# Two moves in a fused attention and MLP kernel: low bits of the weights go from ScalarE to GpSimd, block copies go to more steps

## The chip, the cores and the metric

The kernel runs on one core of a Trainium2 chip. The metric is the device time of one execution, in microseconds (us), as a median of runs. The core's engines run side by side and each takes its own instructions strictly in order: TensorE (PE, with its weight loads, PEld), VectorE (DVE), ScalarE (ACT), GpSimd (POOL), and SyncE (SP), which here only issues DMAs. Before the change the median of three runs is 744.94 us (744.84 to 745.29).

## The reference, cut to what matters

Block-sparse attention over four batches, eight heads, 768 positions, head size 64, and behind it an MLP with squared ReLU over the 3072 tokens.

```python
block, n_blocks, window = 32, 24, 1
scores = scale * np.matmul(q, k.transpose(0, 1, 3, 2))
mask = np.abs(blk_i - blk_j) <= window
mask = mask | (blk_i == 0) | (blk_j == 0) | (blk_i == n_blocks - 1) | (blk_j == n_blocks - 1)
# ... and 3 sampled key blocks for each query block
attn = softmax(where(mask, scores, -1e9));  x = attn @ v
h = np.maximum(x @ w_in, 0.0)          # (3072 x 512) @ (512 x 2048)
return (h * h @ w_out).astype(np.float32)
```

Two things matter here. The first and the last query block see all keys ("whole rows"); the others see a few blocks. And the weights w_in and w_out arrive as float64: each is two 32-bit words, from which the kernel makes fp32 itself.

## The kernel before, in words

The 3072 tokens go through the MLP in eight chunks of 384, and each chunk passes over the 16 blocks f of the hidden dimension. For each f `hidden(c, f)` does twelve matmuls into ph (L883): x and the weight are each cut into a high and a low part, wi holds both parts of the weight, and three products are added. The squared ReLU makes gh and its low part gl (L904 to L917) on ACT, DVE and POOL; `project(c, f)` follows two f later with nine matmuls into po (L936), which need gh, gl and wo. In chunk 0 the projection is plain fp32, three matmuls that the trace shows as six records (L926), and needs only WO and gp.

Between these matmuls stands the attention of the next chunk's tokens, cut into units which are generators: each `yield` hands over to the next step, and a table of lags (`LAG`) says how many steps lie between a unit's parts. A unit of whole rows (class Whole) exists for the batches after the first; twelve of them run, four within each of chunks 1, 3 and 5. Its parts are scores, maxima, exps (pg), the block copies (`move`, L660: sixteen copies of 32x192 elements pg → pgm, even ones by POOL, odd ones by ACT), one transpose by VectorE (L666, pgm → pTg) and the values (pvg, L694). The program's order is each engine's order: no scheduler moves instructions afterwards.

Chunk 0 also makes the weights. For every f and both matrices (part 0 is w_in, which becomes W; part 1 is w_out, which becomes WO) `cut_next` takes four stages in turn, one call every three steps of chunk 0:

- `cut_load` (L785): POOL issues the DMA of 128x1024 32-bit words into craw
- `cut`: ACT makes the rounded top word (L801) and the low bits: it reads the upper 16-bit half of each low word, scales it and writes an integer over the low word (L803)
- `cut_bits`: VectorE shifts and joins both (L812), then the sign (L813); with that W or WO is complete and craw is free
- `cut_split` for a few f only

`split` (L845, L848) makes wi: ACT casts W to the high part (in chunk 0; VectorE in later chunks, L847), and POOL subtracts for the low part. Raw words craw, wi, wo, pg and pgm rotate through one set of seven buffers (tag "w"), so that a new wi waits until an older tenant of its buffer is done; in the middle of chunk 0 that is a craw which `cut_bits` of WO has read. In that stretch ACT, DVE and POOL also carry the attention's exps, maxima (L448), transposed copies (pT), normalisation (rec, xn) and copies of keys into place (L290, L308, L338).

The names in the order of instructions are tile, chunk and f: wi0_7 is wi of chunk 0, f=7; craw8_1 is the raw block of f=8, part 1; pgm1_3 is a unit of whole rows of batch 1.

Of the kernel before, what the change touches and what calls it, by code (L numbers as in the profile page):

```python
# [14 lines left out]
AF = mybir.ActivationFunctionType  # L15
ALU = mybir.AluOpType
# [46 lines left out]
STEP = PIECES // (2 * UC)  # L63
EARLY = 23
LAST = 4
LAG = {"s": 0, "e": 4, "v": 11, "x": 4, "t": 4, "c": 0, "v0": 13, "w0": 4, "w": 19, "n": -1}

G_AT = 6

# [1 line left out]
STEP_1, FIRST_1 = 12, 0  # L71
LAG_1 = {**LAG, "v": 10, "x": 3, "t": 6, "v0": 5, "n": 0}
LAG_0 = {"s": 2, "x": 2, "t": 3, "c": 2, "v0": 2, "n": 2, "r": 1, "l": 3, "l0": 8}
# [23 lines left out]
def tile_block_sparse_attention_moe(ctx: ExitStack, tc, kd, knd, qd, qgd, vd, vnd, samp, const, wcat, out):  # L97
# [9 lines left out]
    nc = tc.nc  # L107
# [14 lines left out]
    below = one.tile([P, 1], F32, name="below")  # L122
# [46 lines left out]
    pool = {}  # L169
# [183 lines left out]
    def load_sampled(k, u, eng, on, which=range(NRAND)):  # L353
        us = halves(k, u)
        if us is None:
            return
        b, t = order[k]
        VA, VB = values_of(k)
        vals = sampled(t, 1, on)
        v4 = columns(vd[b], us).rearrange("(a p) u c -> p a u c", p=BLK)  # L360
        for j in sorted(groups(t)):
            for r in which:
                a = (place(k, j, 3) if r == 2 else 2 + r) * BLK
                dst = (VB if r == 2 else VA)[a : a + BLK, us, j]
                eng.dma_start(dst.unsqueeze(1), v4[:, bass.ds(vals[NRAND * j + r], 1)])
# [215 lines left out]
    class Whole:  # L581
# [71 lines left out]
        def move(self):  # L653

            self.pm = rot.tile([P, NJ, NT, BLK], F32, tag="w", name=f"pgm{self.name}", bufs=WBUFS)
            x = self.p.rearrange("p (k a s) -> p k a s", k=NT, a=NJ)
            for g in range(NJ):
                for a in range(NJ):
                    copy = nc.scalar.copy if a % 2 else nc.gpsimd.tensor_copy
                    copy(self.pm[a * BLK : (a + 1) * BLK, g], x[g * BLK : (g + 1) * BLK, :, a])  # L660
                    if a % 2:
                        yield 0

        def turn_blocks(self):
# [57 lines left out]
    def units(c):  # L722

        halves = [Half(b, t, u) for b, t in order[c * UC : (c + 1) * UC] for u in range(2)]
        wholes = [] if c % 2 else [Whole(c // 2, pr) for pr in range(NPAIR)]
        if c == 0:
            return [(i * STEP_0, u) for i, u in enumerate(wholes + halves)]
        if c == 1:
            return [(i * STEP_1 + FIRST_1, u) for i, u in enumerate(halves)]
        at = begins(c - 1) - EARLY  # L730
        both = [(at + i * STEP, u) for i, u in enumerate(halves)]
        both += [(at + i * STEP + G_AT, u) for i, u in enumerate(wholes)]
        return sorted(both, key=lambda x: x[0])
# [43 lines left out]
    def whole_block(f, part):  # L777
        if part:
            return WO[f]
        return W1[f] if f in SINGLE else rot.tile([P, DM], F32, tag="x", name=f"ct{f}", bufs=5)  # L780

    def cut_load(f, part):
        if wide:
            cv[f, part] = rot.tile([P, DM, 2], I32, tag="w", name=f"craw{f}_{part}", bufs=WBUFS)
            nc.gpsimd.dma_start(cv[f, part].rearrange("p a b -> p (a b)"), wcat[f, part].bitcast(I32))  # L785

    def cut(f, part):

        t = whole_block(f, part)
        if not wide:
            nc.gpsimd.dma_start(t, wcat[f, part])
            cv[f, part] = t
            return
        raw = cv[f, part]  # L800
        nc.scalar.mul(t, raw[:, :, 1].bitcast(F32), 2.0**-112)  # L801
        top = raw.bitcast(U16).rearrange("p a (b c) -> p a b c", c=2)[:, :, 0, 1]
        nc.scalar.activation(raw[:, :, 0], top, AF.Identity, scale=2.0**-13, bias=below)  # L803
        cv[f, part] = raw, t

    def cut_bits(f, part):
# [22 lines left out]
    def cut_next():  # L829

        nonlocal done
        n = len(cuts)
        for stage, lag in ((cut, AHEAD), (cut_bits, AHEAD + 1), (cut_split, AHEAD + 2), (cut_load, 0)):
            if 0 <= done - lag < n:
                stage(*cuts[done - lag])
        done += 1
# [5 lines left out]
    def split(c, src, name):  # L842
        w = rot.tile([P, 2, DM], F32R, tag="w", name=name, bufs=WBUFS)
        if c == 0:
            nc.scalar.copy(w[:, 0], src)  # L845
        else:
            nc.vector.tensor_copy(w[:, 0], src)  # L847
        nc.gpsimd.tensor_tensor(w[:, 1], src, w[:, 0], op=ALU.subtract)  # L848
        return w
# [176 lines left out]
    def prepare():  # L1026
        for k in range(1, UC):
            key_windows(k, 1, nc.vector.tensor_copy)
        for _ in range(AHEAD):
            cut_next()  # L1030
        deque(first, 0)
        for f in windows(1, 0) + windows(1, 1):
            f(nc.gpsimd.tensor_copy)
        load_sampled(1, 0, nc.sync, SP, (2,))
        load_sampled(2, 1, nc.sync, SP, (0, 1))
        deque(copy_keys(0, 2), 0)
# [8 lines left out]
    while work.todo or work.running:  # L1045
        work.step(now)
        now += 1
        ahead = ahead or (later[0] if later else None)
        if now >= KEYS_1 and now % KEYS_N == 0 and later and later[0] is ahead and next(ahead, True):
            later.pop(0)  # L1050
        if now >= FIXED_0 and fixed:
            fixed.pop(0)(nc.scalar.copy)
            if not fixed:
                load_sampled(2, 1, nc.sync, SP, (2,))
        if now == KEYS_0:
            prepare()
        if now >= CUT_0[0] and (now - CUT_0[0]) % CUT_0[1] == 0:
            cut_next()
        if now == SPLIT_0:
            wi1[0, 1] = split(0, W1[1], "wi0_1")  # L1060
    start.__exit__(None, None, None)
    pool["x"] = ctx.enter_context(tc.tile_pool(name="moe", bufs=2, reuse_waits="tile"))
    W1.update({f: pool["x"].tile([P, DM], F32, name=f"W1{f}", bufs=1) for f in SINGLE if f >= W1_LOW})
    WO.update({f: pool["x"].tile([P, DM], F32, name=f"WO{f}", bufs=1) for f in range(WO_LOW, NF)})
    for c in range(1, NCH):
        for at, u in units(c):
            work.add(at, c, lambda u=u, lag=LAG_1 if c == 1 else LAG: u.run(bank, lag))
    now = 0
# [71 lines left out]
```

## Time and profile before

| what | value |
|---|---|
| median of three runs | 744.94 us (744.84 to 745.29) |
| the profiled execution | 745.86 us |
| span of its instructions | 744.0 us |
| TensorE clock granted, mean | 0.991 |
| busy: PE / DVE / ACT / POOL | 714.0 / 533.0 / 500.5 / 539.4 us |
| low bits on ACT (L803) | 32 times, 24.9 us |
| block copies (L660) | 96 on POOL, 36.7 us; 96 on ACT, 33.6 us |
| chunk 0's matmuls | from about 60 to 165 us |

In the profile's rows an arrow reads "out<-in"; a number in square brackets is the idle time of the engine ahead of the row and what ended it. Matmuls overlap each other in the pipeline, so that twelve rows of 0.35 us take about 2.1 us together. "Issue" in the chain of waits is time in which an engine waited for nothing that the profile shows.

### The profile page before, as it was taken

How to read it: one execution, taken by the hardware profiler on the slowest of the kernel's cores; microseconds unless marked ns; L12 is line 12 of the kernel's file. 1: busy time of each engine (PE TensorE's matmuls, PEld its weight loads, DVE VectorE, ACT ScalarE, POOL GpSimd, SP SyncE). 2: the span in 40 equal slices, each digit the busy share in tenths (PEclk: the TensorE clock that was granted, in tenths of full speed). 3: DMA queues.
4: the chain of work that ended last, by engine and by line, in shares of the span. 5: the costliest groups of instructions: out<-in, count | busy, mean ns of one | idle time of the engine just before them, and what ended most of it. 6: DMA issues, size and time to landing. Idle time of an engine off the chain costs nothing.

```text
span 744.0 us, 21519 instructions
## 1 busy us (share of the span) xinstructions
PE 714.0 (96%) x7496; PEld 569.7 (77%) x7496; DVE 533.0 (72%) x1076; ACT 500.5 (67%) x1107; POOL 539.4 (73%) x681
## 2 busy tenths in 40 slices
PE   5869999999999999999999999999999999999997
PEld 2546666567878888877878888877778888888996
DVE  7885766968776877768877786768778686647552
ACT  5875677998875875579776777478866776623222
POOL 7986734249786587769877577877976586868985
PEclk9988999999999999999999999999999999999999
DMA  8785799755555547645455466455355452101001
GB/s 271 226 225 159 206 298 304 179 154 171 146 126 130 174 126 211 145 104 144 104 165 146 100 193 177 132 131 176 95 160 143 100 160 55 34 1 44 1 1 42
DMA packets 94479, 105.22 MB, mean 141 GB/s; under 512 B 13827, under 2 KB 82180, under 8 KB 94372
## 3 DMA queue, kind: packets, MB, share of 16 engines
q1 hardware_dynamic: 88420, 81.00, 41.1%
q0 software_dynamic: 5664, 22.45, 9.2%
q8 instruction: 60, 0.98, 0.6%
q14 instruction: 47, 0.39, 0.2%
q10 hardware_dynamic: 288, 0.39, 0.1%
HBM read 97.50 MB, written 6.29 MB: 140 GB/s over the span
## 4 chain that ended last, share of the span: by engine, by line
PE 72%; DVE 10%; ACT 8%; POOL 5%; issue 3%; DMA 1%; SPq 0%; POOLq 0%; ACTq 0%; DVEq 0%
PE ph L883 30%; PE po L936 26%; PE s L436 5%; PE pv L531 5%; PE po L926 3%; DVE m L448 2%; POOL gl L917 2%; PE pvg L694 2%; POOL pgm L660 1%; ACT craw L803 1%; ACT p L495 1%; POOL wo L848 1%; PE g L624 1%; DVE p L456 1%; DVE pT L487 1%
## 5 line engine op out<-in xcount | busy, mean ns | idle before, releaser
L883 PE MATMUL ph<-xh,wi 128*128 128x384 f32 x960 | 276.1, 348 | 0.6 <-POOL wi L848 0.4
L481 ACT ACTIVATE pm<-p 32x256 f32<-32x256 f32 x528 | 219.3, 415 | 15.4 <-DVE p L456 8.2
L848 POOL TENSOR_TENSOR wi<-W,wi 128x512 fp32r<-128x512 f32 x120 | 163.7, 1364 | 71.8 <-DVE wi L847 36.9
L936 PE MATMUL po<-wo,gh 128*128 128x512 f32 x672 | 211.7, 396 | 0.0
L883 PEld LDWEIGHTS ph<-xh,wi 128*128 128x128 f32 x960 | 173.9, 188 | 23.0 <-issue 10.0
L904 ACT ACTIVATE r<-ph 128x384 f32<-128x384 f32 x128 | 63.0, 492 | 168.2 <-PE ph L883 167.6
L848 POOL TENSOR_TENSOR wo<-WO,wo 128x512 fp32r<-128x512 f32 x112 | 144.9, 1293 | 34.6 <-DVE wo L847 32.9
L917 POOL TENSOR_TENSOR gl<-gf,gh 128x384 fp32r<-128x384 f32 x112 | 119.1, 1063 | 64.1 <-DVE gf L915 54.5
L883 PE MATMUL ph<-xl,wi 128*128 128x384 f32 x480 | 162.4, 338 | 0.0
L936 PEld LDWEIGHTS po<-wo,gh 128*128 128x128 f32 x672 | 123.0, 188 | 27.1 <-issue 7.5
L936 PE MATMUL po<-wo,gl 128*128 128x512 f32 x336 | 134.6, 401 | 5.1 <-POOL gl L917 4.9
L915 DVE SCALAR_TENSOR_TENSOR gf<-ph,r 128x384 f32<-128x384 f32 x112 | 62.0, 553 | 105.7 <-ACT r L904 97.6
L883 PEld LDWEIGHTS ph<-xl,wi 128*128 128x128 f32 x480 | 90.3, 188 | 7.6 <-issue 3.3
L847 DVE CAST wo<-WO 128x512 fp32r<-128x512 f32 x112 | 85.1, 760 | 0.0
L936 PEld LDWEIGHTS po<-wo,gl 128*128 128x128 f32 x336 | 63.0, 187 | 24.6 <-POOL gl L917 11.5
L910 ACT ACTIVATE gh<-r 128x384 fp32r<-128x384 f32 x112 | 59.0, 526 | 10.4 <-ACT r L904 0.4
L448 DVE TENSOR_REDUCE m<-s 128x2 f32<-128x512 f32 (+1 forms) x96 | 61.1, 676 | 3.0 <-PE s L436 3.0
L847 DVE CAST wi<-W 128x512 fp32r<-128x512 f32 x105 | 60.4, 576 | 0.0
L531 PEld LDWEIGHTS pv<-V,pT 128*32 128x32 f32 x2816 | 43.5, 111 | 20.6 <-issue 10.6
L531 PE MATMUL pv<-V,pT 128*32 128x65 f32 x2816 | 52.2, 224 | 5.1 <-DVE xn L548 1.9
L436 PE MATMUL s<-KG,q 64*32 64x256 f32 x1408 | 55.2, 391 | 0.8 <-issue 0.6
L456 DVE TENSOR_TENSOR p<-s,m 128x512 f32<-128x512 f32 (+1 forms) x72 | 45.9, 677 | 0.0
(92 smaller groups left out, 768.1 us busy)
## 6 DMA issues: line engine op xcount, KB each, us to landing
craw<-in_w_dram POOLq DMA_DIRECT2D x32, 512.0 KB, 5.9
V<-in_v_dram SPq DMA_DIRECT2D x462, 32.5 KB, 2.1
KG<-in_k_dram SPq DMA_DIRECT2D x198, 64.0 KB, 1.9
V<-in_v_dram SPq DMA_DIRECT2D x28, 390.0 KB, 5.5
KG<-in_k_dram SPq DMA_DIRECT2D x12, 768.0 KB, 5.9
q<-in_q_dram SPq DMA_DIRECT2D x24, 256.0 KB, 2.8
out_dram<-ot SPq DMA_DIRECT2D x22, 256.0 KB, 5.8
V<-in_v_dram SPq DMA_DIRECT2D x16, 292.5 KB, 6.3
```

Of the source, the lines that this page charges most:

```text
L436: nc.tensor.matmul(self.sb[e][g * BLK : (g + 1) * BLK, i * NSLOT : (i + 1) * NSLOT], q[r, j, pr, :], kg[r, j, :, pr, :], start=True, stop= ...
L448: nc.vector.tensor_reduce(m[at, e], self.sb[e][at].rearrange("p (i c) -> p i c", i=2), axis=AX, op=ALU.max)
L481: nc.scalar.activation(p[a * BLK : (a + 1) * BLK, g], x[g * BLK : (g + 1) * BLK, :, a], AF.Exp, scale=SCALE)
L531: nc.tensor.matmul(po[h * BLK : (h + 1) * BLK, g * VW : (g + 1) * VW], self.pT[:, g, 2 * e + i, c], v[:, self.u, j, h * VW : (h + 1) * VW] ...
L847: nc.vector.tensor_copy(w[:, 0], src)
L848: nc.gpsimd.tensor_tensor(w[:, 1], src, w[:, 0], op=ALU.subtract)
L883: nc.tensor.matmul(ph[c, f][:, :TOK], wi[:, w, cc], x[:, cc], start=(cc == 0 and i == 0), stop=(cc == NCC - 1 and i == 2),)
L904: nc.scalar.activation(r, acc[:, :TOK], AF.Relu)
L910: nc.scalar.activation(gh, r, AF.Square)
L915: nc.vector.scalar_tensor_tensor(gf, acc[:, :TOK], 0.0, r, op0=ALU.max, op1=ALU.mult)
L917: nc.gpsimd.tensor_tensor(gl, gf, gh, op=ALU.subtract)
L936: nc.tensor.matmul(acc[c][u], g[:, at], w[:, k], start=(f == 0 and i == 0), stop=(f == NF - 1 and i == 2))
```

## The change: what it does

```diff
-LAG = {"s": 0, "e": 4, "v": 11, "x": 4, "t": 4, "c": 0, "v0": 13, "w0": 4, "w": 19, "n": -1}
+LAG = {"s": 0, "e": 4, "v": 11, "x": 4, "t": 2, "c": 0, "v0": 13, "w0": 3, "w": 18, "n": -1}
...
                     copy(self.pm[a * BLK : (a + 1) * BLK, g], x[g * BLK : (g + 1) * BLK, :, a])
-                    if a % 2:
+                    if a > 0:
                         yield 0
...
+    low_by = {"pool": False}
...
         top = raw.bitcast(U16).rearrange("p a (b c) -> p a b c", c=2)[:, :, 0, 1]
-        nc.scalar.activation(raw[:, :, 0], top, AF.Identity, scale=2.0**-13, bias=below)
+        if low_by["pool"]:
+            nc.gpsimd.tensor_scalar(raw[:, :, 0], top, 2.0**-13, 2.0**-14 - 0.5, op0=ALU.mult, op1=ALU.add)
+        else:
+            nc.scalar.activation(raw[:, :, 0], top, AF.Identity, scale=2.0**-13, bias=below)
...
+    low_by["pool"] = True
     start.__exit__(None, None, None)
```

The first edit is in `Whole.move` and its lags. The inner loop counts a from 0 to 3: before, a step took two copies (one POOL, one ACT); now the first step of each group of four takes two (a = 0 on POOL and a = 1 on ACT), the second one (POOL) and the third one (ACT). Sixteen copies take twelve steps in place of eight. The lags t, w0 and w are set so that the time from exps to values stays 35 steps: the first copies come two steps earlier, the VectorE transpose one step later.

The second edit moves the low bits from ACT to POOL from the point at which chunk 0 begins; the six that lie ahead of it stay on ACT, 26 move. They read 128x512 16-bit values in steps of 8 bytes, and write 128x512 32-bit integers in steps of 8 bytes.

On POOL in chunk 0, from the subtraction for wi0_6 to that for wi0_8, before:

```order
L848 TENSOR_TENSOR wi0_6_1801<-W16_1368,wi0_6_1801 128x512
L785 DMA craw8_1_1816<-in_w_dram 128x1024
L785 DMA craw11_0_1920<-in_w_dram 128x1024
L848 TENSOR_TENSOR wi0_7_1922<-W17_1369,wi0_7_1922 128x512
L785 DMA craw9_1_1932<-in_w_dram 128x1024
L785 DMA craw12_0_1968<-in_w_dram 128x1024
L178 DMA kn1_1_1988<-in_kn_dram 128x1536
L848 TENSOR_TENSOR wi0_8_1992<-W18_1370,wi0_8_1992 128x512
```

and now:

```order
L853 TENSOR_TENSOR wi0_6_1801<-W16_1368,wi0_6_1801 128x512
L806 TENSOR_SCALAR craw8_0_1537<-craw8_0_1537 128x512
L787 DMA craw8_1_1816<-in_w_dram 128x1024
L806 TENSOR_SCALAR craw6_1_1620<-craw6_1_1620 128x512
L787 DMA craw11_0_1920<-in_w_dram 128x1024
L853 TENSOR_TENSOR wi0_7_1922<-W17_1369,wi0_7_1922 128x512
L806 TENSOR_SCALAR craw9_0_1686<-craw9_0_1686 128x512
L787 DMA craw9_1_1932<-in_w_dram 128x1024
L806 TENSOR_SCALAR craw7_1_1743<-craw7_1_1743 128x512
L787 DMA craw12_0_1968<-in_w_dram 128x1024
L178 DMA kn1_1_1988<-in_kn_dram 128x1536
L853 TENSOR_TENSOR wi0_8_1992<-W18_1370,wi0_8_1992 128x512
```

Two low-bit operations (L806) now stand between two subtractions (L848 before, L853 now), each ahead of a DMA issue. On ACT, at the same place (L801 is L803 now, L845 is L850), before:

```order
L801 ACTIVATE WO6_1381<-craw6_1_1620 128x512
L803 ACTIVATE craw6_1_1620<-craw6_1_1620,below_73 128x512
L845 CAST wi0_7_1922<-W17_1369 128x512
L801 ACTIVATE W19_1371<-craw9_0_1686 128x512
L803 ACTIVATE craw9_0_1686<-craw9_0_1686,below_73 128x512
L520 COPY pT0_4_0_1953<-pt0_4_0_0_1939 128x4x4x32
```

and now:

```order
L909 ACTIVATE r0_6_1960<-ph0_6_1934 128x384
L912 ACTIVATE gp0_6_1962<-r0_6_1960 128x384
L803 ACTIVATE WO7_1382<-craw7_1_1743 128x512
L850 CAST wi0_8_1992<-W18_1370 128x512
L803 ACTIVATE W110_1372<-craw10_0_1779 128x512
```

The cast for the next wi follows the top word of WO at once; the two low-bit operations are gone from it. On POOL in chunk 1, between the subtraction for wi1_8 and gl1_7, where PE waits for gl, before:

```order
L848 TENSOR_TENSOR wi1_8_3641<-W18_1370,wi1_8_3641 128x512
L660 COPY pgm1_3_3514<-pg1_3_3462 32x192 x3
L848 TENSOR_TENSOR wo1_7_3662<-WO7_1382,wo1_7_3662 128x512
L660 COPY pgm1_3_3514<-pg1_3_3462 32x192 x2
L917 TENSOR_TENSOR gl1_7_3693<-gf1_7_3691,gh1_7_3689 128x384
```

and now:

```order
L853 TENSOR_TENSOR wi1_8_3642<-W18_1370,wi1_8_3642 128x512
L660 COPY pgm1_3_3476<-pg1_3_3460 32x192 x2
L853 TENSOR_TENSOR wo1_7_3661<-WO7_1382,wo1_7_3661 128x512
L660 COPY pgm1_3_3476<-pg1_3_3460 32x192
L922 TENSOR_TENSOR gl1_7_3691<-gf1_7_3689,gh1_7_3687 128x384
L660 COPY pgm1_3_3476<-pg1_3_3460 32x192
```

Five copies stood between the two, three do now; one comes behind gl1_7, the other has gone ahead. In chunks 3 and 5 the same piece stands. PE's and SP's orders are the same in both kernels.

## The prediction

> **What bounds the kernel now.** I read the head of the page first, then the busy time by stretch, then the waits of the first chunk, then the chain of waits there, and last the single places that the two edits touch.
>
> ```profile
> PE 714.0 (96%) x7496; PEld 569.7 (77%) x7496; DVE 533.0 (72%) x1076; ACT 500.5 (67%) x1107; POOL 539.4 (73%) x681
> ```
>
> PE is busy for 714.0 of 744.0 us (the span), so an edit that leaves PE's instructions alone, as this one does, can win or lose only where PE stands still. The two edits lie in different places: the low bits in chunk 0 (about 60 to 165 us), the block copies in chunks 1, 3 and 5. The busy time in chunk 0 (PE, PEld, DVE, ACT, POOL, then the clock and the DMA share):
>
> ```profile
> 80.00:100.00 20.00, 19.69 (x198) 12.62 (x197) 13.29 (x25) 14.43 (x29) 12.05 (x28) 1.00 0.80 234
> 100.00:120.00 20.00, 19.82 (x218) 12.99 (x216) 14.13 (x27) 14.68 (x29) 9.47 (x14) 1.00 0.92 282
> 120.00:140.00 20.00, 19.04 (x168) 11.95 (x168) 15.05 (x25) 16.16 (x33) 7.38 (x10) 1.00 0.99 289
> ```
>
> PE idles 0.31, 0.18 and 0.96 us in these. By this view ScalarE is the loaded engine beside PE and POOL has room; but a busy share doesn't tell in which order things follow each other. What waits for what between 56 and 165 us (total us, times, longest):
>
> ```profile
> POOL wi L848 <- ACT wi L845: 32.4, 12, 6.5
> DVE W L812 <- ACT craw L803: 12.8, 10, 2.1
> DVE WO L812 <- ACT craw L803: 12.1, 6, 4.3
> ACT wi L845 <- DVE WO L813: 10.8, 6, 2.8
> ```
>
> That is a ring. VectorE waits for the low bits, ScalarE's next cast of wi waits for VectorE's last bits of WO (its buffer is the one that the raw words leave), POOL waits for the cast. The chain of waits (start, us, what) walks one turn for one f, without POOL in it:
>
> ```profile
> 98.46 0.62 ACT wi L845
> 99.08 0.57 ACT W L801
> 99.65 0.67 ACT craw L803
> ...
> 101.08 0.69 DVE W L813
> 101.77 1.21 DVE m L448 x2
> ...
> 104.59 0.62 ACT wi L845
> ...
> 111.59 0.62 ACT wi L845
> ```
>
> Behind the maxima L448 come the two bit operations for WO, then the next cast. From the cast of f=7 (98.46) to the next (104.59) are 6.13 us; the one after takes 7.00 (to 111.59: four exps come between). Two f: 13.13 us. PE's own beat is seen at its projections (plain fp32, six records a time), of which every second one is:
>
> ```profile
> 83.92 2.84 PE L926 MATMUL po<-WO,gp 128*128 128x512 f32 x6
> 97.78 2.84 PE L926 MATMUL po<-WO,gp 128*128 128x512 f32 x6
> 110.72 2.84 PE L926 MATMUL po<-WO,gp 128*128 128x512 f32 x6
> 124.23 1.98 PE L926 MATMUL po<-WO,gp 128*128 128x512 f32 x4
> ```
>
> The distances are 13.86, 12.94 and 13.51 us, 13.44 in the mean. The least, 12.94, I take as PE's beat without a wait. So ring and PE run almost at one speed: PE loses about 40.31 - 3 x 12.94 = 1.5 us to it, with the 0.96 after 120 us some 2.5 in all. That is all that chunk 0 can give; what it can lose has no such end.
>
> **The change part by part: low bits.** ScalarE loses 26 of its 32 low-bit operations, POOL gets them; two per f. The duration that goes, the rows between which the new one must lie (min/median/max in ns), and POOL's load of raw words (busy us, mean ns; KB, us to landing):
>
> ```profile
> L803 ACT ACTIVATE craw<-craw,below x32: 732/758/1007, 31.7 to 147.3; 128x512 int32<-128x512 uint16 x32
> L338 POOL COPY KG<-kn x18: 604/612/1138, 6.4 to 507.6; 128x512 f32<-128x512 f32 x18
> L848 POOL TENSOR_TENSOR wi<-W,wi x120: 1253/1306/1509, 54.2 to 729.4; 128x512 fp32r<-128x512 f32 x120
> L785 POOL DMA_DIRECT2D craw<-in_w_dram x32 | 17.6, 550 | 14.6 <-ACT WO L801 5.8 <-issue 4.4 <-ACT r L904 4.4
> craw<-in_w_dram POOLq DMA_DIRECT2D x32, 512.0 KB, 5.9
> ```
>
> POOL has no such operation in this trace. Call its duration L. It reads one tensor, as the copy does (0.61 us), but converts from 2-byte to 4-byte integers and does two arithmetic steps, as the copy doesn't; the subtraction reads two tensors (1.27 as a rule). I take L = 0.85, nearer the copy, and keep 0.61 and 1.27 as ends. [...]
>
> Where it stands decides, not how long it is. In POOL's order the low bits of W_(f+2) and of WO_(f-1) come behind the subtraction for wi_f. That subtraction waits for ScalarE's cast; today nothing in the ring waits for the subtraction. After the change it is inside: bits of WO → cast → subtraction → low bits W → low bits WO → bits of WO. And VectorE's bits and POOL can hold each other up:
>
> ```profile
> 137.72 1.42 POOL L848 TENSOR_TENSOR wi<-W,wi 128x512 fp32r<-128x512 f32 x1 [3.53 <-ACT wi L845]
> 138.03 1.66 DVE L813 SCALAR_TENSOR_TENSOR WO<-craw,WO 128x512 int32<-128x512 int32 x1
> ```
>
> L813 takes 0.69 elsewhere; here it ends 0.55 behind POOL's subtraction (139.69 to 139.14), a wait and then its own time. So I let them take turns. [...]
>
> One turn by hand, from the end of the WO bits as 0: cast from 0.08 to 0.78 with its handover (row 98.46); subtraction to 2.06 (1.28); low bits of W to 2.06 + L; VectorE L812 to 2.8 + L, while POOL issues its load (0.55 us); low bits of WO, ahead of L813, to 2.83 + 2L; L813 to 3.55 + 2L. On an even f the WO bits follow at once: 4.98 + 2L. On an odd f the maxima (1.21 and 0.06) stand between: 6.25 + 2L. Two f: 11.23 + 4L, or 11.17 + 3L if VectorE wins the turn and one low operation hides behind L813.
>
> - L = 0.85: 14.63 (13.72 if VectorE wins). L = 0.61: 13.67. L = 1.27: 16.31.
> - Against the 13.44 of now, 0.85 gives +1.19 for two f. Break-even lies at L = 0.55, or 0.76 where VectorE wins.
>
> ScalarE's relief, 2 x 0.67 per f on the chain, is already in this sum: its two steps left the ring, and 1.28 + 2L came in. The ring holds from the cast for f=5 to the WO bits of f=11, some 6.6 turns or 3.3 pairs: +3.9 us. Behind f=11 it is slack (the last raw loads are through), and PE's delay stays.
>
> Ahead of that, POOL has no gap around f=4 and 5, when it still copies keys:
>
> ```profile
> 78.27 1.27 POOL L848 TENSOR_TENSOR wi<-W,wi 128x512 fp32r<-128x512 f32 x1 [0.52 <-ACT wi L845]
> ...
> 86.01 1.31 POOL L848 TENSOR_TENSOR wi<-W,wi 128x512 fp32r<-128x512 f32 x1
> ```
>
> Between these subtractions it is busy through 7.7 us, with two low operations to come: wi_5 is late by up to 2L = 1.7 us. Part of that delay is in the ring's sum already, so I count 1.4 (ends 0.6 and 1.8; 1.2 goes with L = 0.61). Chunk 0: +5.3 us; ends +2 (L = 0.61, with 0.23 x 3.3 and 1.2) and +11 (L = 1.27: 2.87 x 3.3 and 1.8). The DMA loads are issued by POOL just behind its low bits, at most 2L = 1.7 us later for a W; a load is issued two to three turns of 6 us ahead of its first use, against 5.9 us of landing, so they stay covered; without that cover the first late one would cost the same 1.7.
>
> **The change part by part: block copies.** The sixteen copies of a whole-rows unit (eight POOL, eight ACT) go to twelve steps, starting two steps earlier; their number and PE's order stay. Where PE waits for POOL's gl, at f=7 of chunk 3 (the same in 1 and 5, at 207.82 and 551.52):
>
> ```profile
> 375.09 1.10 POOL L660 COPY pgm<-pg 32x192 f32<-32x192 f32 x3
> 376.27 1.29 POOL L848 TENSOR_TENSOR wo<-WO,wo 128x512 fp32r<-128x512 f32 x1
> 377.63 0.91 POOL L660 COPY pgm<-pg 32x192 f32<-32x192 f32 x2
> 378.62 0.99 POOL L917 TENSOR_TENSOR gl<-gf,gh 128x384 fp32r<-128x384 f32 x1
> 379.67 0.50 PE L936 MATMUL po<-wo,gl 128*128 128x512 f32 x1 [1.15 <-POOL gl L917]
> ```
>
> Five copies stand between the subtraction for wi_8 and gl_7 now, three after it. So gl_7 starts 1.10/3 + 0.91/2 = 0.82 us earlier, and of PE's 1.15 us remain 0.33, if the rest arrives: ACT's r_7 has two copies of 0.35 fewer before it. Three times: -2.5 us. PE's waits for gl in sum, and ACT's copy:
>
> ```profile
> PE po L936 <- POOL gl L917: 4.9, 8, 1.1
> L660 ACT COPY pgm<-pg x96: 347/350/356, 151.8 to 546.7; 32x192 f32<-32x192 f32 x96
> ```
>
> Of the 4.9 us, 3.4 are these three; the other five are 1.5, on neighbouring f, where copies leave as well as arrive: I count -0.5, and +0.4 for one f where a copy of ACT (0.35) moves ahead of r. Together -2.6; ends 0 (another input of gl is as late) and -3.9 (all of it and the restart of PE behind each wait).
>
> **Sum.** +5.3 - 2.6 = +2.7 us on the profiled execution's 745.86: 748.6. The median of the runs is 0.92 below it (744.94), so 747.6.
>
> **The rivals.**
>
> (a) *The other side: ScalarE is what limits chunk 0.* For it: 24.9 us of VectorE's waits name ScalarE's low bits, and POOL is busy for 7 to 9.5 of 20 us. If the low operations fit into gaps of POOL, the ring falls under PE's 12.94 and PE's 2.5 us of waits go: -2.5 - 2.6 = -5.1, 739.8. The point from which it decides is L = 0.43 (11.23 + 4L = 12.94), or 0.59 where VectorE wins all turns. Against it: 0.59 is under the copy of POOL, 0.61.
>
> (b) *Ring and gain cancel.* L near 0.65 with turns going either way: the ring 13.12 to 13.83, so -1.0 to +1.3 over 3.3 pairs, 1.2 ahead of it, and the copies -2.6: 742.5 to 744.8, say 744.0.
>
> [...]
>
> (d) *The copies bring nothing*, since gf or wo arrives as late as gl's place in the queue: +5.3 alone, 750.2. In the rows above POOL goes from copy to copy with no idle shown, which speaks against.
>
> **How the numbers follow.** Forecast 0.42; (a) 0.17; (b) 0.21; (c) 0.10; (d) 0.10. 0.2% of 744.94 is 1.5 us, about what a measurement of this kernel tells from no change; same is 743.45 to 746.43. Forecast: mostly slower (0.32 of its 0.42), 0.08 same, 0.02 faster. (a) all faster. (b) 0.12 same, 0.09 faster. (c) and (d) 0.18 slower, 0.02 same. Sum: faster 0.28, same 0.22, slower 0.50. The likeliest alone (L from 0.72 to 0.98) gives 745.8 to 749.5; the range for 8 in 10 takes in (b), (d) and most of (c), and the nearer half of (a): 740.5 to 751.5.
>
> **What would show it.** In the changed profile: the low operation on POOL at 0.8 to 0.9 us; VectorE's wait in L812 named after POOL; the projections in chunk 0 some 14.6 us apart for two f; chunk 1 starting about 5 us later; PE's waits for gl at f=7 of 0.3 in place of 1.15. It is wrong if POOL's operation is under 0.6 us, if the projections stay 13 apart, or if PE's waits for gl are as they were.

## The result, and the profile after

The changed kernel takes 749.2 us (median of 6 runs, 748.62 to 749.66) against 745.16 us before (744.84 to 746.11): a ratio of 1.0051, 95% interval 1.0038 to 1.0064, some 4 us slower. Forecast were 747.6 us, 740.5 to 751.5, and slower as the likeliest. The profiled execution took 749.19 us, with a span of 747.4, against 745.86 and 744.0. So way and range came out right; of the terms, only some did.

The head of the page, and the busy time in chunk 0 (PE, PEld, DVE, ACT, POOL, clock, DMA share), of the changed kernel:

```profile
PE 714.1 (96%) x7496; PEld 570.3 (76%) x7496; DVE 544.5 (73%) x1076; ACT 483.7 (65%) x1081; POOL 559.0 (75%) x707
```

```profile
80.00:100.00 20.00, 17.88 (x171) 12.09 (x177) 13.08 (x23) 9.92 (x22) 16.25 (x33) 1.00 0.69 201
100.00:120.00 20.00, 19.25 (x243) 12.50 (x228) 13.47 (x23) 10.37 (x21) 11.89 (x16) 1.00 0.97 290
120.00:140.00 20.00, 17.48 (x150) 10.49 (x149) 13.73 (x26) 10.33 (x23) 12.75 (x18) 1.00 0.99 304
```

PE's work is the same (714.1). ScalarE fell from 14.4 to 9.9 us of the first stretch, and nobody was the faster for it: PE's idle time in the three stretches rose from 1.45 to 5.39 us. The new operation, and among the longest waits between 56 and 170 us (total us, times, longest):

```profile
L806 POOL TENSOR_SCALAR craw<-craw x26: 644/660/1365, 59.3 to 148.9; 128x512 int32<-128x512 uint16 x26
```

```profile
DVE W L817 <- POOL craw L806: 22.1, 9, 4.9
ACT wi L850 <- DVE rec L545: 19.8, 4, 5.7
...
PE s L436 <- DVE xn L548: 3.8, 2, 2.1
```

The duration L that the prediction put at 0.85 is 0.66 us in the median (min/median/max in ns; the longest, 1365, from 143.59 us on, ran beside VectorE's bits, L817 and L818 at 143.74 and 144.44 us). And a wait that it didn't have stands in the last row: PE's scores wait for VectorE's xn, 2.1 us once. PE's plain projections, the same ones as in the rows of before:

```profile
87.87 2.84 PE L931 MATMUL po<-WO,gp 128*128 128x512 f32 x6
100.81 2.84 PE L931 MATMUL po<-WO,gp 128*128 128x512 f32 x6
114.54 2.84 PE L931 MATMUL po<-WO,gp 128*128 128x512 f32 x6
128.42 1.98 PE L931 MATMUL po<-WO,gp 128*128 128x512 f32 x4
```

They follow each other at 12.94, 13.73 and 13.88 us, 40.55 in all, where before had 40.31. But the first of them (f=3) already stands 3.95 us later than before. The table gives the shift of the projections' starts against before, from the timelines, for the changed kernel and for the experiments below (a positive number is later). The projection of f=10 is split around the scores, and its column is the second piece; those of f=14 and f=15 stand in one row. Each line is one profiled execution, and f=0 shows by how much it was early or late already at the start, which has to be taken off:

| run | f=0 | f=3 | f=5 | f=7 | f=9 | f=10, rest | f=14, 15 |
|---|---|---|---|---|---|---|---|
| the change | 0.14 | 3.95 | 3.03 | 3.82 | 4.19 | 5.06 | 5.08 |
| copies alone | -0.22 | -0.21 | -0.33 | -0.32 | -0.31 | -0.11 | -0.08 |
| low bits alone | -0.61 | 3.73 | 4.04 | 3.80 | 3.61 | 4.50 | 6.22 |
| early ones on ScalarE | -0.90 | -0.41 | -0.70 | -0.69 | -0.24 | 0.63 | 2.35 |
| only early ones on POOL | -1.28 | 2.72 | 3.26 | 3.03 | 2.17 | 2.16 | 2.18 |
| attention first | 0.40 | 0.40 | 2.11 | 2.39 | 2.21 | 2.59 | 2.62 |
| in four pieces | -0.40 | 5.06 | 5.22 | 7.80 | 10.17 | 11.79 | 11.82 |
| POOL busy beside | -0.18 | 0.23 | 6.93 | 6.69 | 5.68 | 4.03 | 4.06 |
| W only | -0.22 | 3.67 | 4.22 | 3.99 | 3.38 | 4.04 | 4.03 |
| WO only | -0.33 | 0.30 | 1.43 | 1.60 | 1.47 | 1.39 | 1.42 |
| WO only, from f=5 | 0.60 | 0.61 | 0.20 | -0.03 | -1.04 | -0.81 | -0.78 |
| the same, attention first | 0.16 | 0.17 | -0.97 | -1.20 | -2.21 | -3.87 | -3.84 |
| attention first, all on ScalarE | 0.96 | 0.97 | 0.02 | 0.03 | 0.03 | -0.06 | -0.03 |

Chunk 0 costs 5.08 us, close to the forecast's 5.3. Behind it, by the starts of ScalarE's r, the shift goes from 5.08 to 4.27 in chunk 1, to 3.86 in chunk 3 and to 3.42 in chunk 5; in chunks 2, 4, 6 and 7 it stays. So the copies gain 1.7 us, where 2.6 were forecast.

How the 3.95 us come about: POOL between the subtractions for wi_4 and wi_5, then VectorE, then PE, all of the changed kernel.

```profile
79.96 1.27 POOL L853 TENSOR_TENSOR wi<-W,wi 128x512 fp32r<-128x512 f32 x1
81.18 1.11 POOL L290 COPY KG<-kn 128x64 f32 x6
82.24 0.92 POOL L308 COPY KG<-kn 128x192 f32<-128x192 f32 x3
83.11 0.58 POOL L290 COPY KG<-kn 128x64 f32 x3
83.78 0.64 POOL L806 TENSOR_SCALAR craw<-craw 128x512 int32<-128x512 uint16 x1
```

```profile
84.46 0.69 DVE L817 SCALAR_TENSOR_TENSOR W<-W,craw 128x512 int32<-128x512 int32 x1 [4.92 <-POOL craw L806]
85.18 0.78 DVE L818 SCALAR_TENSOR_TENSOR W<-craw,W 128x512 int32<-128x512 int32 x1
85.88 0.15 DVE L545 TENSOR_SCALAR rec<-pv 128x4 f32<-128x4 f32 x1
86.07 0.18 DVE L546 RECIPROCAL rec<-rec 128x4 f32<-128x4 f32 x1
86.28 0.42 DVE L548 TENSOR_TENSOR xn<-pv,rec 128x256 f32<-128x256 f32 x1
```

```profile
86.85 1.09 PE L436 MATMUL s<-KG,q 64*32 64x256 f32 x30 [2.12 <-DVE xn L548]
```

The low bits of W for f=6 stand behind twelve key copies; VectorE waits 4.92 us for them; rec and xn, which have nothing to do with weights, are queued behind the two bit operations; and PE's next scores wait for xn. Before, ScalarE had these bits ready 5 us earlier, and rec started at 80.78 us. The same happens once ahead of it, in small: at 76.36 us PE's values have waited 0.50 us for pT, which stands on VectorE behind bits of W that waited 3.53 us for POOL, and the projection of f=2 starts 0.98 us late. From there to f=3 another 2.97 us are lost.

### The profile page after: what moved, and what is told of

Its sections match the earlier page's. It is cut to its first block, busy times and chain, and to the rows that moved or that the text cites. A ratio compares the mean times of both kernels' runs of the same rounds, so it can differ in the third digit from the quotient of the medians.

```text
span 747.4 us, 21506 instructions
## 1 busy us (share of the span) xinstructions
PE 714.1 (96%) x7496; PEld 570.3 (76%) x7496; DVE 544.5 (73%) x1076; ACT 483.7 (65%) x1081; POOL 559.0 (75%) x707
## 4 chain that ended last, share of the span: by engine, by line
PE 72%; DVE 11%; POOL 7%; ACT 5%; issue 4%; DMA 1%; POOLq 0%; ACTq 0%; DVEq 0%
PE ph L888 30%; PE po L941 27%; PE s L436 5%; PE pv L531 5%; PE po L931 2%; DVE m L448 2%; PE pvg L694 2%; POOL KG L290 1%; PE g L624 1%; POOL wi L853 1%; DVE W L818 1%; POOL gl L922 1%; POOL craw L806 1%; DVE p L456 1%; DVE pT L487 1%
## 5 line engine op out<-in xcount | busy, mean ns | idle before, releaser
L853 POOL TENSOR_TENSOR wi<-W,wi 128x512 fp32r<-128x512 f32 x120 | 163.5, 1362 | 53.9 <-DVE wi L852 36.1
L853 POOL TENSOR_TENSOR wo<-WO,wo 128x512 fp32r<-128x512 f32 x112 | 145.3, 1297 | 33.8 <-DVE wo L852 31.8
L852 DVE CAST wi<-W 128x512 fp32r<-128x512 f32 x105 | 64.6, 615 | 0.0
```

## The experiments

Each comparison is against runs of the kernel before on the same chip. Two theories stood at the start. EARLY: chunk 0 loses its time while f=3 to f=5 are made, where the low bits wait among the key copies (as projections follow two f later, this shows at f=3 in the table). RING, the prediction's larger term: the ring with the subtraction and two low operations in it is slower over all turns up to f=11.

**The parts by themselves.**

```diff
+LAG = {..., "t": 2, "c": 0, "v0": 13, "w0": 3, "w": 18, "n": -1}
...
+                    if a > 0:
                         yield 0
...
```

> Only the block copies are spread; ScalarE makes all low bits. Theory (the edits add): chunk 0 as before, chunks 1 to 7 as in the changed kernel, 1.7 us less: 743.5 us. Rival (the gain of the copies hangs on chunk 0's new timing): 745.2 us, or anything but 743.5. In the profile: PE's wait for gl at f=7 of chunks 1, 3 and 5 about 0.33 us each in place of 1.14, and chunks 3 and 5 0.4 us slower ahead of it.

Measured: 744.13 us, ratio 0.9972 (0.9961 to 0.9984). Faster, 0.6 us above the expected number; by the starts of r the shift falls from 0.00 to -0.79 in chunk 1, to -1.18 in chunk 3 and -1.35 in chunk 5. The other half:

```diff
...
+            nc.gpsimd.tensor_scalar(raw[:, :, 0], top, 2.0**-13, 2.0**-14 - 0.5, op0=ALU.mult, op1=ALU.add)
...
```

> Only the low bits move to POOL; the block copies are as before. Theory (the edits add): chunk 0 is 5.1 us longer, the rest as before: 750.3 us. Rival (the sum is not additive, part of chunk 0's delay is won back later by looser engines): under 749.5 us.

Measured: 750.29 us, ratio 1.0061 (1.0048 to 1.0074), the expected number. By the ratios the two parts' -2.1 and +4.5 us add up to +2.4, the whole has +3.8; with intervals of about 1 us each that is no contradiction, and behind chunk 0 the shifts show the copies' gain in the changed kernel (-1.7) and with the copies alone (-1.4), and none with the low bits alone (6.17 to 6.01). (The profiled execution of the low bits alone took 751.79 us, 1.5 above its median; the clock has a part in its line of the table, see below.)

**Where in chunk 0.** The first six operations (W of f=4 to 6, WO of f=2 to 4) stay on ScalarE.

```diff
-        if low_by["pool"]:
+        if low_by["pool"] and f + 2 * part >= 7:
```

> As the changed kernel, but the first six low-bit operations of chunk 0 (W of f=4 to 6, WO of f=2 to 4), which stand among POOL's copies of keys, stay on ScalarE; twenty are on POOL. Theory EARLY (the low bits wait behind the key copies, VectorE's bits for them, rec and xn behind these, PE's scores for xn): the 4.0 us that chunk 0 loses between f=3 and f=5 go, the ring stays: 745.2 us and 0 to +1. Rival RING (the ring with POOL's two operations in it costs the time, over all turns from f=5 to f=11): 748 to 749 us.

Measured: 745.84 us, ratio 1.0000 (0.9991 to 1.0009). EARLY's number. In the table the shift stays between -0.41 and -0.70 up to f=7. Behind it the ring does show: from f=7 to f=9 it is 13.96 us, 13.51 before, and then PE waits 1.71 us for xn at 133 us. Copies alone have 744.13 us on the same chip, so the twenty later operations still cost 1.7 us; in the profiled execution part of the loss is the clock (below). The mirror image:

```diff
+        if low_by["pool"] and f + 2 * part < 7:
```

> The mirror image of the run that left the early ones on ScalarE: of the changed kernel's low bits on POOL only the first six (W of f=4 to 6, WO of f=2 to 4) stay there, the twenty later ones go back to ScalarE. Theory EARLY: the 3 to 4 us of f=3 to 5 are lost here too, at most 1 us comes back behind it, since PE's beat and the old ring are nearly equal: 747 to 748 us (before: 745.4). Rival RING: as with the copies alone, 744 us.

Measured: 747.08 us, ratio 1.0022 (1.0012 to 1.0033). Six operations in the wrong place bring 2.7 us at f=3, 4.0 counted from f=0, and the changed kernel's wait is in the trace again (2.11 us for xn). About 1 us comes back later, as expected.

**What is queued behind the wait.** In each step of chunk 0 the attention's part goes ahead of the weights'; the same operations stay on POOL.

```diff
-            if c == 0 and now % CUT_1 == 0 and done < len(cuts) + AHEAD + 2:
-                cut_next()
             if now < begins(c + 1) - LAST:
                 work.step(now)
             else:
                 work.step(now)
                 work.drain(c + 1, now)
+            if c == 0 and now % CUT_1 == 0 and done < len(cuts) + AHEAD + 2:
+                cut_next()
```

> As the changed kernel, but in each step of chunk 0 the attention's part is written ahead of the weights' part, so that on VectorE rec and xn stand ahead of the bits for W of f=6, not behind them; the number of instructions is the same. Theory EARLY: PE's wait of 2.1 us for xn at f=4 goes, 2 to 3 us less than the changed kernel: 746 to 747 us. Rival RING: 749.2 us as it was.

Measured: 745.62 us, ratio 0.9995 (0.9986 to 1.0004), 0.4 us below the expected range. The wait for xn at f=4 is gone and the shift at f=3 falls from 3.95 to 0.40 us. Instead PE waits 1.14 us for wi at 88.66 us, and the shift is 2.11 us at f=5: the subtraction for wi_5 starts at 87.33 us in place of 86.01, 1.32 us later, as much as POOL's two extra operations of 0.66 take. That is the mechanism that the prediction had for this place.

**Waiting, or POOL's load?** ScalarE makes the low bits; POOL does idle work at the same 26 places.

```diff
...
+            for _ in range(3):
+                nc.gpsimd.tensor_scalar(xx, src, 2.0**-13, 2.0**-14 - 0.5, op0=ALU.mult, op1=ALU.add)
...
+        nc.scalar.activation(raw[:, :, 0], top, AF.Identity, scale=2.0**-13, bias=below)
```

> As the changed kernel, but ScalarE makes all low bits again; POOL, at the same 26 places, does three operations of 128x64 on other data (some 0.7 us in all) whose result is not used, so that POOL is as busy and VectorE doesn't wait for it. Theory (it is the waiting for POOL, not POOL's load, that costs): as with the copies alone, 744 to 745 us. Rival (POOL's load delays the subtractions and key copies, or its operations hold VectorE up): 748 to 749.5 us.

Measured: 749.13 us, ratio 1.0053 (1.0033 to 1.0073). The theory that only the waiting costs falls. POOL and PE:

```profile
88.62 1.40 POOL L809 TENSOR_SCALAR xx<-W 128x64 int32<-128x64 uint16 x3
90.08 0.58 POOL L787 DMA_DIRECT2D craw<-in_w_dram  x1
90.69 1.28 POOL L855 TENSOR_TENSOR wi<-W,wi 128x512 fp32r<-128x512 f32 x1
```

```profile
92.02 1.01 PE L890 MATMUL ph<-xh,wi 128*128 128x384 f32 x2 [4.68 <-POOL wi L855]
```

POOL has no room among the key copies: without VectorE's wait the subtraction for wi_5 starts at 90.69 us in place of 86.01, and PE waits for it directly. (Three pieces of idle work take 0.89 us and up to 1.76 where they run beside VectorE's bits, more than 0.66, and the eighteen key copies between the two subtractions take 6.8 us, 4.3 in the changed kernel, so the size is overstated; the clock has a part in the 6.93 us as well, see below.) Behind it, though, nothing more is lost: the projections of f=6, 8 and 10 stand at 110.74, 123.45 and 135.72 us, and the shift falls from 6.93 to 4.06. So POOL's load costs in the crowded place. That in the ring it is the waiting is not shown by this run: PE is late there, and the ring has that much slack.

**The ring's law.** Each low operation is cut into four: the same work in four instructions of 0.307 us in the median, in place of one of 0.66.

```diff
+            for at in range(0, DM, 128):
+                nc.gpsimd.tensor_scalar(raw[:, at : at + 128, 0], top[:, at : at + 128], 2.0**-13, 2.0**-14 - 0.5, ...)
...
```

> As the changed kernel, but each low-bit operation on POOL is cut into four of 128x128, which does the same work and makes L longer by three setups: about 1.2 us in place of 0.66. If the ring is the sum of the prediction, its period for two f is 11.23 + 4L = 16.0 us in place of 13.7 (14.8 where VectorE wins a turn), 3.3 pairs: +4 to +8 us, and +1 to +1.6 ahead of it: 754 to 759 us. If the ring isn't what limits f=5 to 11: only the part ahead, 750 to 751 us.

Measured: 756.2 us, ratio 1.0148 (1.0126 to 1.0170), 11 us slower. POOL in one turn, and PE's projections of f=5 and f=7:

```profile
106.77 1.45 POOL L807 TENSOR_SCALAR craw<-craw 128x128 int32<-128x128 uint16 x4
108.28 0.61 POOL L787 DMA_DIRECT2D craw<-in_w_dram  x1
108.96 1.73 POOL L807 TENSOR_SCALAR craw<-craw 128x128 int32<-128x128 uint16 x4
```

```profile
103.00 2.84 PE L934 MATMUL po<-WO,gp 128*128 128x512 f32 x6
...
118.52 2.84 PE L934 MATMUL po<-WO,gp 128*128 128x512 f32 x6
```

The period is 15.52 us, the next one (f=7 to f=9) 15.88. With L = 1.45, read from the first row, the prediction's walk gives 11.17 + 3 x 1.45 = 15.5 where VectorE gets in between, 17.0 where it doesn't; with four pieces at their median of 0.307 us (L = 1.23) 14.9 and 16.2. The ring is real, and the walk sizes it within these bounds; at L = 0.66 it gives 13.15 to 13.87, and 13.73 and 13.88 were measured. ScalarE's casts of the changed kernel bound one even and one odd turn:

```profile
94.92 0.62 ACT L850 CAST wi<-W 128x512 fp32r<-128x512 f32 x1 [5.69 <-DVE rec L545]
...
101.08 0.62 ACT L850 CAST wi<-W 128x512 fp32r<-128x512 f32 x1 [2.00 <-DVE WO L818]
...
108.65 0.62 ACT L850 CAST wi<-W 128x512 fp32r<-128x512 f32 x1 [4.41 <-DVE rec L545]
```

They are 6.16 and 7.57 us; the walk has 4.98 + 2 x 0.66 = 6.30 and 6.25 + 2 x 0.66 = 7.57.

**One matrix on POOL.**

```diff
+        if low_by["pool"] and part == 0:
```

> The copies spread; POOL makes the low bits of W only (thirteen), ScalarE those of WO. By the prediction's walk with one L = 0.66 in a turn: cast to 0.78, subtraction to 2.06, low bits of W to 2.72, four bit operations to 5.56, with the maxima 6.83: 12.4 us for two f, under PE's 12.94, so the ring costs nothing. But W of f=6 still waits behind the key copies, and rec and xn behind it: the 3 us of f=3 to 5 stay. 746.5 to 747.5 us. Rival (two operations between the key copies are needed for that wait): 744 to 745 us.

Measured: 748.33 us, ratio 1.0036 (1.0022 to 1.0050). The ring is free (102.00 to 114.71, 12.71 us for f=5 to f=7); the loss of f=3 stays (3.67 us). It is 0.8 us above the expected range; in the profiled execution PE's clock has a part in the time (below).

```diff
+        if low_by["pool"] and part == 1:
```

> The copies spread; POOL makes the low bits of WO only (thirteen), ScalarE those of W. The same walk: subtraction to 2.06, low bits of WO to 2.72 while VectorE does W's bits to about 3.5, WO's bits to 4.9, with the maxima 6.15: 11.05 us for two f, under PE's 12.94. rec and xn stand behind W's bits, which ScalarE feeds as before, so the wait for xn at f=4 goes; three operations (WO of f=2 to 4) still make the key copies and the subtraction for f=5 later by 0.7 to 1.4 us: 744 to 745.5 us. Rival (any operation on POOL among the key copies costs the 3 us): 747 us.

Measured: 745.89 us, ratio 1.0008 (0.9999 to 1.0017), 0.4 us above the expected bounds. The wait for xn at f=4 is gone, waits for wi of 0.33 and 0.51 us are there. W's and WO's operations, though equal in size, aren't equal in place: at f=4 rec stands behind W's bits.

**Towards a better version.** Two things follow: keep POOL free until the key copies are through, and only one operation per turn behind the subtraction.

```diff
+        if low_by["pool"] and part == 1 and f >= 5:
```

> The copies spread; POOL makes the low bits of WO from f=5 on (ten), behind the key copies; ScalarE makes all others. Ring 11.05 us for two f, nothing between the key copies: PE's waits between f=5 and f=11 (1 to 1.5 us) go: 742.5 to 743.5 us, where the copies alone have 744.0. Rival (PE's beat, not the ring, set the time there, or VectorE and POOL hold each other up as much as is won): 744.0 to 744.5 us.

Measured: 743.19 us, ratio 0.9969 (0.9960 to 0.9978). Within the expected range, but by time not told apart from the copies alone (0.9972); in the table chunk 0 ends 0.7 us earlier than theirs. The wait at 131 us is still there (1.42 us). Attention first by itself, all low bits on ScalarE:

> The copies spread, all low bits on ScalarE, and in each step of chunk 0 the attention's part ahead of the weights' part. Theory: what was left of PE's waits in chunk 0 is the scores at 131 us, whose bank is freed by xn behind the bits of WO; with xn ahead of the bits this wait of 1.4 us goes: 742.5 to 743.5 us. Rival: ring and bits are later by what xn takes on VectorE (1.2 us with rec and the transpose) and it comes out even or worse: 744 to 746 us.

Measured: 743.95 us, ratio 0.9976 (0.9966 to 0.9986): no gain over the copies alone, though the last wait falls from 1.44 to 0.71 us; the expected range was missed by 0.4 us. (Counted from f=0 the profiled execution's chunk 0 is 1.1 us shorter than theirs; the medians don't show it.) Both together:

> As the run with POOL making the low bits of WO from f=5 on, and in each step of chunk 0 the attention's part ahead of the weights' part, so that xn and rec stand ahead of the bits. If the scores' wait for xn at 131 us is what is left: 742 to 743 us. Rival: the order only shifts VectorE's work, no difference to the run without it.

Measured: 741.05 us (738.95 to 742.63), ratio 0.9947 (0.9932 to 0.9963). That is 0.9 us below the expected range and beats both kernels, the one before by 4 us, of which the copies alone make about 2. PE in chunk 0, and the projections of f=3, 5 and 7:

```profile
60.00:165.00 105.00, 104.85 (x999) 71.14 (x1000) 76.83 (x136) 77.93 (x162) 61.75 (x107) 0.99 0.76 224
```

```profile
84.09 2.84 PE L931 MATMUL po<-WO,gp 128*128 128x512 f32 x6
...
96.81 2.84 PE L931 MATMUL po<-WO,gp 128*128 128x512 f32 x6
...
109.52 2.84 PE L931 MATMUL po<-WO,gp 128*128 128x512 f32 x6
```

PE stands still for 0.15 of 105 us (before: 1.59). Its beat is 12.72 us there, and 12.50 from f=7 to f=9.

## Why the prediction was right, and where it was not

- **Chunk 0, +5.3: measured +5.08, by other terms than forecast.** The sum hit by errors of opposite sign, which is luck. With the copies the profiled executions differ by 3.3 us, where 2.7 were forecast. Of the signs that the prediction names, chunk 1 some 5 us later, L812's wait for POOL and gl's 0.3 us came; 0.8 to 0.9 us for the operation and 14.6 us for two f did not.
- **The ring, +3.9: too large.** "I take L = 0.85, nearer the copy": it is 0.66, nearer still. The walk itself holds: with 0.66 it gives up to 13.87 us for two f, and 13.73 and 13.88 were measured (the period from f=3 to f=5, 12.94, lies behind the early delay, and no wait of PE for wi stands in it). It is no law for every pair, since a late PE gives the ring slack: from f=5 on, the pairs of the other runs with whole operations for both matrices on POOL lie between 12.70 and 13.96 us. (What it calls low bits of WO_(f-1) is WO_f in the order; the sum doesn't depend on it.) Against before's 13.44 that makes 1.3 to 1.4 over three pairs; in the shifts between f=3 and f=9 only 0.24 remain of it.
- **Ahead of it, +1.4: too small, and the failed step.** "wi_5 is late by up to 2L" holds in the attention-first run (1.32 us); in the changed kernel wi_5 is 2.22 us late (86.01 to 88.23), as the subtraction for wi_4 is already 1.69 us late. But the step looked only at the subtraction. It didn't ask what VectorE has queued behind the bits for W of f=6, which wait for POOL behind twelve copies: rec and xn, and PE's scores behind them. 3.95 us at f=3, 0.14 of them there from the start, in place of 1.4. The attention-first run takes that wait away and with it 3.5 us at f=3; 1.7 us are lost again by f=5, where the subtraction counts.
- **Behind f=11, nothing: +0.9.** PE's scores, at 131 us before and 137 us now, wait for xn, 1.70 us after the change; xn again stands behind bits, and these waited 2.39 us for POOL. The forecast counted this wait among what chunk 0 can win, not what it can lose.
- **PE's beat, 12.94: too high.** The least distance in a trace in which the ring is as slow as PE isn't PE's own; it is at most 12.72, and 12.50 for the last pair. Chunk 0 had about 4 us to give, not 2.5, as the last experiment shows (-3.84). And "only where PE stands still" was too narrow: of these 4 us only 1.4 were idle time of PE (1.59 to 0.15). The rest lay in rows that count as busy, such as eight transposes (L510) that take 1.38 us at 94.05 us before and 1.04 in the last experiment; what stretches them is not shown.
- **The copies, -2.6: measured -1.7 in the shifts.** The three waits for gl at f=7 came out at 0.33 us each, as forecast. PE's restart behind such a wait, which the end of -3.9 counts in, is some 0.1 us: in the trace of before gl's matmul takes 0.50 us there, against a median of 0.397. The 0.4 us for a copy of ACT ahead of r came, but twice, in chunks 3 and 5; and the 0.5 us at neighbouring f didn't come. There gh is now late, and gl behind it:

```profile
515.31 0.73 PE L941 MATMUL po<-wo,gh 128*128 128x512 f32 x2 [0.50 <-ACT gh L915]
516.46 0.50 PE L941 MATMUL po<-wo,gl 128*128 128x512 f32 x1 [0.42 <-POOL gl L922]
...
554.95 0.49 PE L941 MATMUL po<-wo,gl 128*128 128x512 f32 x1 [0.33 <-POOL gl L922]
```

- **The rivals.** (a), ScalarE as the limit, is out for this change: it was relieved, and PE waited more. Its idea isn't: with the attention first, eleven low-bit operations less on ScalarE bring 743.95 to 741.05 us. (b) had L about right (0.65) and was wrong by what it shared with the forecast: the stretch ahead of the ring, the wait for xn behind it, and the copies' 2.6. No run shows the 1.1 us for L that go with (c): it is 0.66 in the median, and only two of the 26 are longer than 1.1 (1.15 and 1.37, both beside VectorE's bits). (d) is out by the waits for gl.

## What to carry to other kernels

When an operation moves to an engine with idle time, ask in which stretch that idle time lies, and then what each waiting engine has queued behind the instruction that will wait: the dearest item here was a normalisation that only stood behind it. Two operations of one kind are not one price: late and for one matrix, with the attention written first, the move of low bits wins 2 to 3 us over the copies alone (741.05 against 744.13; ratios 0.9947 and 0.9972), where all of it at once loses 4.5. A beat read off a trace in which everything runs at one speed is an upper bound.

## What was not expected of the hardware

After some of its waits PE ran at a clock of 0.50. In the run with the early ones on ScalarE, from the wait of 1.71 us ahead of 133.05 us on (clock in the column behind POOL):

```profile
133.00:135.00 2.00, 1.95 (x23) 1.15 (x24) 0.31 (x1) 2.00 (x6) 1.87 (x2) 0.89 1.02 256
135.00:138.00 3.00, 3.00 (x6) 1.39 (x5) 2.89 (x4) 2.35 (x5) 1.53 (x4) 0.50 1.09 233
138.00:141.00 3.00, 3.00 (x21) 2.75 (x20) 2.97 (x6) 0.95 (x3) 2.84 (x3) 1.00 0.46 141
```

The clock is 0.50 for more than 3 us, and 1.7 us more are lost between the second piece of f=10's projection and f=11's (6.31 us against 4.60 before). The run with W only shows it behind its wait of 2.11 us; the changed kernel, with waits of 2.12 and 1.70 us, shows 1.00 from 64 us on. The same stretch of both, W only first:

```profile
84.00:94.00 10.00, 7.89 (x107) 4.09 (x106) 9.55 (x16) 3.81 (x7) 6.85 (x14) 0.83 0.59 174
```

```profile
84.00:94.00 10.00, 7.88 (x117) 5.05 (x116) 8.90 (x15) 3.15 (x6) 9.13 (x16) 1.00 0.54 174
```

A mean of 0.83 over 10 us is 3.4 us at 0.50. The low bits alone (behind waits of 2.13 and 1.73 us), only the early ones on POOL (2.11) and the run in four pieces (2.87, but not behind its 2.43) show such stretches too, each of about 3.4 us, and POOL busy beside one of twice that, behind its 4.68 us (0.81 over 84 to 102 us). So the wait of 1.71 us cost about twice its length (1.7 us more), which not every execution shows, and the lines of these six runs in the table can hold up to 1.7 us of such loss for each stretch; what decides it stays open.
